# Decode attention and MLP on one core: K1 and V1 are requested in two halves, V1's first half after half of V0

## The chip, the core and the metric

The kernel runs on one core of a Trainium2 chip. The core has a matrix engine (TensorE, PE in the profile, with its weight loads as PEld), a vector engine (VectorE, DVE), a scalar engine (ScalarE, ACT), GpSimd (POOL) and SyncE (SP), which here does nothing but request transfers. Each engine runs its own list of instructions and waits on semaphores. Transfers between the chip's memory and the core's on-chip memory (128 partitions) are done by 16 DMA engines.

The metric is the time of one execution on the device in microseconds (us), the median of several runs.

## The reference

One token is decoded: a layer norm, attention with 32 heads over a cache of 32768 keys and values of 128 numbers each, and a small MLP, each with a residual. Everything is bf16.

```python
def _A_ref(x, k_cache, v_cache, wq, wo):
    B, Sq, D = x.shape            # 1, 1, 512
    H, Dh = 32, 128
    q = (x @ wq).reshape(B, Sq, H, Dh) transposed to (0, 2, 1, 3)
    scores = jnp.einsum("bhqd,bhkd->bhqk", q, k_cache) * (Dh ** -0.5)
    p = _softmax(scores, axis=-1)
    o = jnp.einsum("bhqk,bhkd->bhqd", p, v_cache)
    return o transposed back, reshape(B, Sq, H * Dh) @ wo

def _B_ref(x, w1, b1, w2):        # 512 -> 1376 -> 512
    h = jnp.einsum("bsd,df->bsf", x, w1) + b1
    sp = jnp.log1p(jnp.exp(-jnp.abs(h))) + jnp.where(h > 0, h, jnp.zeros_like(h))
    return jnp.einsum("bsf,fd->bsd", h * jnp.tanh(sp), w2)

h = x + _A_ref(_layernorm(x), k_cache, v_cache, wq, wo)
h2 = h + _B_ref(_layernorm(h), w1, b1, w2)
```

Keys and values of one head are 32768 x 128 x 2 bytes = 8.39 MB each, so the 32 heads read 537 MB.

## The kernel before

**Where data lives.** `ring` holds six slots of 32 KB a partition. Slots 0 and 1 are the home of the keys of even heads, 2 and 3 of odd heads, 4 and 5 of the values of every head. Partition p holds 256 consecutive keys (or values) of a head, "rows" 0 to 255 below, which lie in one run of 64 KB in the chip's memory. The query weights WQ (4.2 MB) lie in slot 4 at the start, so V0 can be requested only when the queries are computed; the output weights WO take the place of the keys of head 30 at the end.

**Requests.** SP goes through a list written out at L446 to L449: WQ, K0, K1, V0, K2, V1, K3, V2, and so on to WO, V31 and the MLP's weights. For each entry it waits until the place is free (L540: for K(h), until TensorE has used K(h-2); for V0, until it has used WQ) and, for V(h) with h > 0, until V(h-1) has been used (L565). `done_with` (L503) names the event waited for: for values it is `pv{h}_64` or `pv{h}_128` if the piece ends at row 64 or 128, and otherwise `pv{h}`, the end of the product with the values. Everything is requested on SP, in this order, and goes into one queue.

**Pieces.** `pieces` (L427) says into which pieces an entry is cut. Before, K0 is cut at row 128 (two pieces with 32 KB a partition), V31 into six pieces, and every other K and V is one transfer with 64 KB a partition. The first piece adds 16 to the semaphore `ready` of the home when it has landed, each later one adds 16 to a semaphore of its own cut, in `cut_sems`. For heads without that cut, SP adds the missing counts itself (L568, L569; `uncut`, L435, says for which heads and how many), so that TensorE, whose code is a loop over heads, can wait for the same count in every round.

**TensorE's rounds.** For each head `head` (L735) runs 32 groups of eight rows: eight transposes of 128 x 128 (L666), a copy by VectorE out of the accumulation memory (L672), and, three groups later, eight products with the query (L642). Then VectorE takes the maximum (L706). `rest` (L746) for head t, after the keys of head t+1, runs C (the sum, L727), the product with the values in four stretches `pv` of rows 0 to 63, 64 to 127 and 128 to 255 (L693; below "pv(t)"), with the next head's small steps A (L712) and B (L717) between them, and `oev`. For head 0 there is a block of its own, `turn` (L741): A0, B0 and the exponential of head 0 stand right after the keys of head 0. So the order on TensorE is keys(0), turn, keys(1), pv(0), keys(2), pv(1), keys(3), and so on. All heads but the first pass run the same instructions again: the loop's blocks are `head` and `rest`.

**What the change touches.** `pieces` (L427 to L430), the semaphores beside L452, the loop on SP that requests keys and values (L561 to L569), and the waits of B in `soft_b` (L716 to L718). A wait named `keys_in` (L76 to L80) makes TensorE wait at the first row of a head's keys until `ready` of that home has its count, 16 per head.

Of the kernel before, what the change touches and what calls it, by code (L numbers as in the profile page):

```python
# [291 lines left out]
def bass_sequential_preLN__mha_block_cached__dense_activation_mish__decode_kernel(  # L292
    nc: bass.Bass,
    A_x: bass.AP,
    A_k_cache: bass.AP,
    A_v_cache: bass.AP,
    A_wq: bass.AP,
    A_wo: bass.AP,
    B_x: bass.AP,
    B_w1: bass.AP,  # L300
    B_b1: bass.AP,
    B_w2: bass.AP,
    out: bass.AP,
):
    build_kernel(nc, A_x, A_k_cache, A_v_cache, A_wq, A_wo, B_w1, B_b1, B_w2, out)


def build_kernel(nc, A_x, A_k_cache, A_v_cache, A_wq, A_wo, B_w1, B_b1, B_w2, out):
# [3 lines left out]
    H = HD // Dh  # L312
# [9 lines left out]
    TPS = 128  # L322
# [19 lines left out]
    def sb(shape, dt, name):  # L342
        cm = nc.sbuf_tensor(name, shape, dt)
        t = cm.__enter__()
        allocs.append(cm)
        return t.ap()
# [21 lines left out]
    gmax = sb([1, 1], F32, "gmax")  # L368
# [39 lines left out]
    sem = nc.alloc_semaphore  # L408
# [3 lines left out]
    ready = [sem(f"ready{i}") for i in range(NS)]  # L412
# [12 lines left out]
    CUTS = {"k": [TPS], "v": [TPS // 2, TPS, 192, 224, 240]}  # L425

    def pieces(what):  # L427
        kind, h = what
        at = CUTS[kind] if what in (("k", 0), ("v", H - 1)) else []
        return list(zip([0] + at, at + [SCOLS]))  # L430

    def cut_at(kind, h, r):
        return r in [r0 for r0, _ in pieces((kind, h))]

    def uncut(what):  # L435


        kind, h = what
        for r in CUTS[kind]:
            if not cut_at(kind, h, r) and (h == 0 or cut_at(kind, h - 1, r)):  # L440
                n = 1
                while h + n < H and not cut_at(kind, h + n, r):
                    n += 1
                yield r, n
# [5 lines left out]
    cut_sems = {k: {r: sem(f"cut_{k}_{r}") for r in CUTS[k]} for k in CUTS}  # L450

    s_wl = sem("wl")  # L452
    w1_sems = [sem(f"w1_{n}") for n in range(len(W1P))]
    w2_sems = [sem(f"w2_{n}") for n in range(len(W2P))]

# [5 lines left out]
    def slot_of(what):  # L461
        if what in HOMES:
            return HOMES[what]
        if what[0] in ("w1", "w2"):
            return HOMES[WL]
        return V_HOME if what[0] == "v" else what[1] % 2 * HALVES
# [6 lines left out]
    def ready_wait(what):  # L473
        if what == WL:
            return (s_wl, 16)
        return (ready[slot_of(what)], 16 * fills[what])

    def free_name(what):
        return "free" + "_".join(map(str, what))

    def freed_by(what):
        if what == WO:
            return done_with("k", H - 2, 0, SCOLS)
        if what[0] == "k" and what[1] > 1:
            return done_with("k", what[1] - 2, 0, SCOLS)
        if what == ("v", 0):
            return [free_name(WQ)]
        return []

    def tiles_of(what):  # L490
        return ring[:, slot_of(what):slot_of(what) + HALVES, :].rearrange("p s (r d) -> p (s r) d", d=Dh)

    def keys_of(cache, h):
        return cache[0, h, :, :].rearrange("(p r) d -> p r d", r=SCOLS)
# [8 lines left out]
    def done_with(kind, h, r0, r1):  # L503
        if kind == "v":
            return [f"pv{h}_{r1}" if r1 in V_EVENTS else f"pv{h}"]
        return [free_name(("k", h, half)) for half in range(HALVES) if r0 < (half + 1) * TPS and r1 > half * TPS]
# [15 lines left out]
    def program(S):  # L522
# [3 lines left out]
        v = nc.vector  # L526
# [4 lines left out]
        def start(dst, src, s):  # L531
            S.dma(SP, lambda: sp.dma_start(dst, src).then_inc(s, 16))  # L532
# [3 lines left out]
        for what in order:  # L536
            slot = slot_of(what)
            if what == ("k", 1):
                S.stay(SP)
            S.wait(SP, freed_by(what))  # L540
            flat = ring[:, slot, :]
            if what[0] == "wq":
                S.wait(SP, ["b1z"])
                start(b1r[0:FJ, :], B_b1[0:FJ * 128].rearrange("(j p) -> j p", j=FJ), s_b1)
                start(b1r[FJ:FJ + 1, 0:FLAST], B_b1[FJ * 128:F].rearrange("(o p) -> o p", o=1), s_b1)
            elif what[0] == "wo":
                start(flat, A_wo.rearrange("(p j) n -> p (j n)", j=32), ready[slot])
            elif what == WL:
                start(wol_v, A_wo[(H - 1) * Dh:H * Dh, :], s_wl)
            elif what[0] == "w1":  # L550
                k = what[1]
                start(w1_v[:, k, :], B_w1[k * 128:(k + 1) * 128, :], w1_sems[k])
            elif what[0] == "w2":
                n = what[1]
                if n + 1 < len(W2_J):
                    j0, j1 = W2_J[n], W2_J[n + 1]
                    start(w2_v[:, j0:j1, :], B_w2[j0 * 128:j1 * 128, :].rearrange("(j p) n -> p j n", p=128), w2_sems[n])
                else:
                    start(w2_v[0:FLAST, FJ, :], B_w2[FJ * 128:F, :], w2_sems[n])
            else:  # L560
                kind, h = what  # L561
                rows = keys_of(A_k_cache if kind == "k" else A_v_cache, h)
                for r0, r1 in pieces(what):
                    if kind == "v" and h:
                        S.wait(SP, done_with(kind, h - 1, r0, r1))  # L565
                    start(tiles_of(what)[:, r0:r1, :], rows[:, r0:r1, :], cut_sems[kind][r0] if r0 else ready[slot])

                for r, n in uncut(what) if kind == "v" else [(r, H - 1) for r in CUTS["k"] if h == 2]:  # L568
                    S.dma(SP, lambda r=r, n=n: sp.sem_inc(cut_sems[kind][r], 16 * n))  # L569
        S.dma(SP, lambda: sp.dma_start(out[0, 0, :].rearrange("(c m) -> c m", c=KC), outr[0:128:32, :]).then_inc(s_out, 16),  # L570
              waits=["fin"])
# [20 lines left out]
        for c in range(2 * KC):  # L592
            cols = xr[0:1, c:D:KC] if c < KC else xr[0:1, (c - KC) * 128:(c - KC + 1) * 128]
            S.step(PE, lambda c=c, cols=cols: t_.matmul(X_REG[:, c:c + 1], cols, identb[0:1, 0:1], start=True, stop=True),
                   name=("xT" if c == 2 * KC - 1 else None), waits=(["identb", (s_x, 16)] if c == 0 else ()))
# [22 lines left out]
        for h in range(H):  # L618
            for kc in range(KC):
# [3 lines left out]
                       name=(["q", free_name(("wq",))] if last else None),  # L623
                       waits=(["xn0", ready_wait(("wq",))] if h == 0 and kc == 0 else ()))
# [90 lines left out]

        def soft_b(h):  # L716
            S.step(PE, lambda: t_.matmul(B_REG, onesm[0:1, :], gmax[:, :], start=True, stop=True),  # L717
                   name=f"B{h}", waits=[f"gmax{h}", "consts0"], kind="B")  # L718
            S.step(DVE, lambda: v.tensor_scalar_mul(nb[:, :], B_REG, -SC), name=f"nb{h}", waits=[f"B{h}"], kind="nb")  # L719

        def soft_exp(h):
# [19 lines left out]
        def turn():  # L741
            soft_a(0)
            soft_b(0)
            soft_exp(0)

        def rest(i):  # L746
            t = i - 1
            soft_c(t)
            pv(t, 0, TPS // 2)
            S.unless_final(PE, "soft_a", lambda: soft_a(i))  # L750
            pv(t, TPS // 2, TPS)
            S.unless_final(PE, "soft_b", lambda: soft_b(i))
            pv(t, TPS, SCOLS)
            oev(t)
            if t < H - 1:
                soft_exp(i)
# [84 lines left out]
    log = {}  # L841
    counted = _Sched(nc, False, events, sems, log)
    program(counted)
    nc.sync.dma_start(ring[:, slot_of(WQ), :], A_wq.rearrange("(p k) n -> p (k n)", k=KC)).then_inc(ready[slot_of(WQ)], 16)
    with nc.Block() as block:
        for eng_name, attr in ((POOL, "gpsimd"), (SP, "sync"), (DVE, "vector"), (ACT, "scalar"), (PE, "tensor")):
            emitter = _Sched(nc, True, events, sems, log, only=eng_name)

            def _run(eng, emitter=emitter):
                program(emitter)  # L850
            getattr(block, attr)(_run)
            assert emitter.cnt == counted.cnt
# [31 lines left out]
```

## Time and profile before

| what | value |
|---|---|
| time, median of 3 runs | 1281.71 us (1281.58 to 1282.12) |
| the profiled execution | 1281.4 us, span of its instructions 1279.6 us |
| mean granted TensorE clock | 0.769 |
| busy: PE, DVE, ACT | 1019.0 us (80%), 716.1 us (56%), 20.8 us (2%) |
| read from the chip's memory | 548.21 MB, 428 GB/s over the span |
| requests of V0, K2, V1, V2 on SP | 16.59, 56.28, 95.31, 127.90 us |

The page divides the span in 40 slices of 32 us; a digit is the busy share in tenths. In the chain of waits each row is a start, a length and what was done or waited for; "issue" is time in which an engine waited for nothing that the profile shows. A row of the windows gives, for a stretch of time, its length, the busy time of PE, PEld, DVE, ACT and POOL with the number of instructions, the granted clock, the share of the DMA engines and the rate in GB/s. In the DMA view, q1 is the queue of SP's transfers and q8 carries instructions; a row gives packets, MB and the share of the 16 engines' time. In the list of waits the numbers are the total, how often, and the longest.

### The profile page before, as it was taken

The page shows a single profiled execution, that of the slowest core. Times are in us where ns is not written, and L with a number is a line of the kernel's source. Part 1 is how long each engine was busy: PE and PEld are TensorE (multiplying, and loading weights), DVE is VectorE, ACT ScalarE, POOL GpSimd, SP SyncE. Part 2 cuts the span into 40 slices and gives each one's busy share as a digit, 9 for nine tenths or more (in the row PEclk, how much of TensorE's full clock was granted, in tenths as well). Part 3 has the DMA queues.
Part 4 walks back from the last instruction along what each step waited for, and adds up shares of the span by engine and source line. Part 5 has one row for each costly group of instructions (what it writes and reads, how often), then busy time and mean ns, then how long its engine had stood idle before and what let it go on. Part 6 is the DMA issues. An engine that isn't in the chain of part 4 may idle for free.

```text
span 1279.6 us, 54437 instructions
## 1 busy us (share of the span) xinstructions
PE 1019.0 (80%) x25044; PEld 992.2 (78%) x25044; DVE 716.1 (56%) x1252; ACT 20.8 (2%) x71; POOL 0.8 (0%) x8
## 2 busy tenths in 40 slices
PE   3699777788777798777797777897777887777987
PEld 3699777788777798777797777897777887777885
DVE  2566654466654566545566544666445666445661
ACT  0000000000000000000000000000000000000000
POOL 0000000000000000000000000000000000000000
PEclk9888777788777788767788776888677887767885
DMA  9979999999999999999999999999999999999998
GB/s 425 420 339 426 445 440 426 426 426 459 426 426 426 449 436 426 426 426 459 426 426 426 453 432 426 426 434 451 426 426 426 457 428 426 426 436 449 426 426 355
DMA packets 12584, 548.35 MB, mean 429 GB/s; under 512 B 1343, under 2 KB 2848, under 8 KB 3616
## 3 DMA queue, kind: packets, MB, share of 16 engines
q1 hardware_dynamic: 12574, 548.22, 99.3%
q8 instruction: 8, 0.13, 0.0%
q10 hardware_dynamic: 2, 0.00, 0.0%
HBM read 548.21 MB, written 0.00 MB: 428 GB/s over the span
## 4 chain that ended last, share of the span: by engine, by line
DMA 55%; DVE 23%; PE 18%; SPq 2%; issue 2%; POOL 0%; POOLq 0%
DMA ring<-in_A_k_cache_dram 54%; DVE ering L672 23%; PE ops L693 9%; PE tps L666 7%; SPq L532 2%; PE sps L642 1%; PE hlp L717 1%; PE hlp L712 1%; DMA ring<-in_B_w_dram 1%; PE hlp L727 0%; PE tps L829 0%; DVE pmax L706 0%; DVE outr L834 0%; DVE gmax L714 0%; SPq L68 0%
## 5 line engine op out<-in xcount | busy, mean ns | idle before, releaser
L666 PE MATMUL tps<-identb,ring 128*128 128x128 bf16 x8192 | 671.1, 233 | 218.4 <-DMA ring<-in_A_k_cache_dram 214.5
L672 DVE COPY ering<-tps 128x1024 bf16<-128x1024 bf16 x1024 | 669.7, 692 | 274.5 <-PE tps L666 274.1
L666 PEld LDWEIGHTS tps<-identb,ring 128*128 x8192 | 524.3, 104 | 221.1 <-issue 221.1
L642 PE MATMUL sps<-qcur,ering 128*128 128x1 bf16 x8192 | 343.9, 164 | 11.3 <-DVE ering L672 6.6
L642 PEld LDWEIGHTS sps<-qcur,ering 128*128 128x128 bf16 x8192 | 309.9, 97 | 14.2 <-DVE ering L672 9.4
L693 PEld LDWEIGHTS ops<-pbuf,ring 128*128 128x128 bf16 x8192 | 226.4, 103 | 15.7 <-issue 12.4
L693 PE MATMUL ops<-pbuf,ring 128*128 128x1 bf16 x8192 | 231.1, 165 | 3.1 <-DMA ring<-in_A_v_cache_dram 2.5
L701 DVE TENSOR_TENSOR oT<-ops,rtotc 128x1 f32 x31 | 5.0, 161 | 107.8 <-PE ops L693 107.8
L714 DVE TENSOR_REDUCE gmax<-hlp 1x1 f32<-1x128 f32 x32 | 8.9, 278 | 63.4 <-PE hlp L712 63.4
L719 DVE TENSOR_SCALAR nbias<-hlp 128x1 f32<-128x1 f32 x32 | 5.1, 158 | 63.5 <-PE hlp L717 63.5
L722 ACT ACTIVATE pbuf<-sps,nbias 128x256 bf16<-128x256 f32 x32 | 15.2, 475 | 1229.4 <-PE ops L693 1171.7
L706 DVE TENSOR_REDUCE pmax<-sps 128x1 f32<-128x256 f32 x32 | 13.6, 425 | 14.3 <-PE sps L642 14.3
L712 PE MATMUL hlp<-ident,pmax 128*1 128x128 f32 x64 | 17.2, 365 | 3.5 <-issue 3.5
L717 PE MATMUL hlp<-gmax,onesmat 1*128 1x1 f32 x64 | 18.5, 356 | 0.4 <-DVE gmax L714 0.4
L717 PEld LDWEIGHTS hlp<-gmax,onesmat 1*128 1x128 f32 x64 | 15.8, 304 | 1.3 <-DVE gmax L714 0.9
L727 PE MATMUL hlp<-esum,onesmat 128*128 128x1 f32 x64 | 12.3, 261 | 5.3 <-issue 2.8
L727 PEld LDWEIGHTS hlp<-esum,onesmat 128*128 128x128 f32 x64 | 9.8, 192 | 7.9 <-issue 7.9
L621 PE MATMUL hlp<-xnT,ring 128*128 128x1 bf16 x128 | 3.5, 165 | 9.1 <-DMA ring<-in_A_wq_dram 9.1
L621 PEld LDWEIGHTS hlp<-xnT,ring 128*128 128x128 bf16 x128 | 3.5, 104 | 9.2 <-issue 9.2
L729 DVE RECIPROCAL rtotc<-hlp 128x1 f32<-128x1 f32 x32 | 5.4, 168 | 4.2 <-PE hlp L727 2.4
L625 DVE CAST qT<-hlp 128x32 bf16<-128x32 f32 x1 | 0.2, 192 | 11.4 <-PE hlp L621 11.4
L722 ACT ACTIVATION_READ_ACCUMULATOR pbuf<-sps,nbias 128x1 f32 x32 | 6.2, 194 | 0.0
(75 smaller groups left out, 37.9 us busy)
## 6 DMA issues: line engine op xcount, KB each, us to landing
ring<-in_A_k_cache_dram SPq DMA_DIRECT2D x2, 4096.0 KB, 26.6
ring<-in_A_v_cache_dram SPq DMA_DIRECT2D x3, 2048.0 KB, 11.3
ring<-in_A_wq_dram SPq DMA_DIRECT2D x1, 4096.0 KB, 12.1
ring<-in_A_wo_dram SPq DMA_DIRECT2D x1, 4096.0 KB, 35.3
ring<-in_B_w_dram SPq DMA_DIRECT2D x4, 344.0 KB, 16.8
ring<-in_A_v_cache_dram SPq DMA_DIRECT2D x1, 1024.0 KB, 14.3
ring<-in_A_v_cache_dram SPq DMA_DIRECT2D x2, 512.0 KB, 15.5
ring<-in_B_w_dram SPq DMA_DIRECT2D x1, 640.0 KB, 16.9
```

Source lines behind the costliest of these rows:

```text
L532: S.dma(SP, lambda: sp.dma_start(dst, src).then_inc(s, 16))
L621: S.step(PE, lambda h=h, kc=kc: t_.matmul(Q_REG[:, h:h + 1], wq_v[:, kc, h * Dh:(h + 1) * Dh], xnT[:, 0, kc:kc + 1], start=(kc == 0), stop ...
L642: S.step(PE, lambda r=r: t_.matmul(S_ps[:, col0 + r:col0 + r + 1], ering[:, bg % NE, r, :], qcur[:, :], start=True, stop=True), name=(name ...
L666: S.step(PE, lambda r=r, at=at: t_.matmul(tb[:, r * 128:(r + 1) * 128], key_tile(S, at), identb[:, :], is_transpose=True, start=True, stop ...
L672: S.step(DVE, lambda: v.tensor_copy(ering[:, bg % NE, :, :].rearrange("p r d -> p (r d)"), tb[:, :]), name=f"ev{bg}", waits=[f"trb{bg}"], ...
L693: S.step(PE, lambda r=r: t_.matmul(o_ps[:, 0:1], vt[:, r, :], pbuf[:, r:r + 1], start=(r == 0), stop=(r == SCOLS - 1)), name=(names or Non ...
L706: S.step(DVE, lambda: v.tensor_reduce(pmax[:, :], S_ps[:, 0:SCOLS], AXX, ALU.max), name=f"pmax{h}", waits=[f"qkh{h}"], kind="pmax")
L712: S.step(PE, lambda: t_.matmul(A_REG, pmax[:, :], ident[:, :], start=True, stop=True), name=f"A{h}", waits=[f"pmax{h}", "ident", f"rcp{h - ...
L714: S.step(DVE, lambda: v.tensor_reduce(gmax[:, :], A_REG, AXX, ALU.max), name=f"gmax{h}", waits=[f"A{h}"], kind="gmax")
L717: S.step(PE, lambda: t_.matmul(B_REG, onesm[0:1, :], gmax[:, :], start=True, stop=True), name=f"B{h}", waits=[f"gmax{h}", "consts0"], kind ...
L722: S.step(ACT, lambda: a.activation(pbuf[:, :], S_ps[:, 0:SCOLS], ACTF.Exp, bias=nb[:, :], scale=SC, accum_out=esum[:, :]), name=f"exp{h}", ...
L727: S.step(PE, lambda: t_.matmul(C_REG, onesm[:, :], esum[:, :], start=True, stop=True), name=f"C{h}", waits=[f"exp{h}"], kind="C")
```

## The change

K1 and V1, one transfer each before, become two with 32 KB a partition. For K1 the first half (rows 0 to 127) adds to a new semaphore `s_k1`, the second to `ready`; TensorE waits for `s_k1` ahead of B0, in the block that runs once. V1's first half waits for `pv0_128`, the product with V0's rows 0 to 127, and adds to `ready`; its second half waits for `pv0`, the end of the product, and adds to the semaphore of the cut at row 128. The counts that SP adds for that cut are then made for head 0 beside V0 and for heads 2 to 30 beside V2, since head 1 has a transfer of its own there.

```diff
     def pieces(what):
         kind, h = what
-        at = CUTS[kind] if what in (("k", 0), ("v", H - 1)) else []
+        at = CUTS[kind] if what in (("k", 0), ("k", 1), ("v", H - 1)) else [TPS] if what == ("v", 1) else []
         return list(zip([0] + at, at + [SCOLS]))
...
     s_wl = sem("wl")
+    s_k1 = sem("k1")
...
                     if kind == "v" and h:
                         S.wait(SP, done_with(kind, h - 1, r0, r1))
-                    start(tiles_of(what)[:, r0:r1, :], rows[:, r0:r1, :], cut_sems[kind][r0] if r0 else ready[slot])
+                    if what == ("k", 1):
+                        s = ready[slot] if r0 else s_k1
+                    else:
+                        s = cut_sems[kind][r0] if r0 else ready[slot]
+                    start(tiles_of(what)[:, r0:r1, :], rows[:, r0:r1, :], s)
...
         def soft_b(h):
             S.step(PE, lambda: t_.matmul(B_REG, onesm[0:1, :], gmax[:, :], start=True, stop=True),
-                   name=f"B{h}", waits=[f"gmax{h}", "consts0"], kind="B")
+                   name=f"B{h}", waits=[f"gmax{h}", "consts0"] + ([] if h else [(s_k1, 16)]), kind="B")
```

## The prediction

> **What bounds the kernel now.** I read the page's slices first, to see which resource is full and where it is not.
>
> ```profile
> span 1279.6 us, 54437 instructions
> DMA  9979999999999999999999999999999999999998
> GB/s 425 420 339 426 445 440 426 426 426 459 426 426 426 449 436 426 426 426 459 426 426 426 453 432 426 426 434 451 426 426 426 457 428 426 426 436 449 426 426 355
> ```
>
> The 16 DMA engines are full in every slice but the third (64 to 96 us) and the last. So the kernel is a stream of 548 MB, and its time is that stream plus whatever time the engines stand empty. The list of waits agrees: TensorE waits for keys once in nearly every head.
>
> ```profile
> PE tps L666 <- DMA ring<-in_A_k_cache_dram: 214.5, 30, 8.8
> ```
>
> These 30 waits, 7.2 us each on average, are TensorE's spare time per head. Next, the chain of waits in order of time, which gives the landings of keys and the place where the stream is held up.
>
> ```profile
> 1.96 21.93 DMA ring<-in_A_k_cache_dram
> ...
> 34.57 2.25 issue
> ...
> 41.86 4.62 issue
> ...
> 57.80 3.06 issue
> ...
> 61.81 0.58 PE hlp L717 x2
> ...
> 88.74 1.80 PE ops L693 x64
> ...
> 91.51 0.59 issue
> 92.10 3.19 PE ops L693 x114
> 95.31 0.33 SPq L532
> ...
> 95.75 40.67 DMA ring<-in_A_k_cache_dram
> ...
> 1175.44 44.77 DMA ring<-in_A_k_cache_dram
> ```
>
> Start plus length is the landing: K0's first half at 23.89 us, K3 at 136.42, K31 at 1220.21. From K3 to K31 lie 56 transfers of 8.39 MB in 1083.8 us: 19.35 us each, 433 GB/s, with no loss. From K0's first half to K3 lie 5.5 transfers (K0's other half, K1, V0, K2, V1, K3): at 19.35 they take 106.4 us and K3 would land at 130.3. It lands **6.1 us** later. That is all that any better order near the start can win; the rest of the span is the stream itself.
>
> Where the 6.1 us go is seen in half-microsecond windows (last column GB/s, the one before it the DMA share; a packet counts where it begins).
>
> ```profile
> 87.00:87.50 0.50, 0.50 (x25) 0.50 (x22) 0.00 (x0) 0.00 (x0) 0.00 (x0) 0.50 3.03 1311
> 88.50:89.00 0.50, 0.50 (x14) 0.33 (x13) 0.22 (x1) 0.00 (x0) 0.00 (x0) 0.50 1.51 655
> 89.00:89.50 0.50, 0.50 (x25) 0.50 (x23) 0.06 (x1) 0.00 (x0) 0.00 (x0) 0.50 0.30 131
> 90.00:96.00 6.00, 4.69 (x151) 4.51 (x147) 0.32 (x2) 0.57 (x2) 0.00 (x0) 0.50 0.00 0
> 96.00:96.50 0.50, 0.35 (x4) 0.36 (x5) 0.00 (x0) 0.00 (x0) 0.00 (x0) 0.50 3.95 1311
> 96.50:97.00 0.50, 0.50 (x8) 0.50 (x6) 0.00 (x0) 0.00 (x0) 0.00 (x0) 0.50 1.77 655
> 97.00:97.50 0.50, 0.50 (x7) 0.50 (x6) 0.28 (x1) 0.00 (x0) 0.00 (x0) 0.50 0.32 131
> ```
>
> 1311 GB/s in 0.5 us is ten 64 KB packets, 655 five, 131 one: the last packet of each of the 16 engines for K2, and the first of each for V1. At 433 GB/s over 16 engines a 64 KB packet takes 2.42 us, so ten engines run dry near 89.7, five near 91.2, one near 91.7, and they resume at 96.25, 96.75 and 97.25: (10 x 6.6 + 5 x 5.6 + 5.6)/16 = 6.2 us empty on average. Two views give the same loss. V1 comes late because it is asked for at 95.31, when V0's last product has ended at 95.29; its packets begin 0.8 us after.
>
> **The change, part by part.** *V1 in two halves.* The first needs only the products of V0's rows below 128. Those end at 88.74 + 1.80 = 90.54, so SP asks at 90.56 instead of 95.31: **4.75 us** earlier. The second half is asked for at pv(0)'s end, about 95.3, behind 9.7 us of the first half (half of 19.35): no gap. On TensorE the wait of pv(1) at row 128 becomes one on a real transfer: V1 as a whole now lands near 111 us (K2's 91.7 and 19.35). Row 128 of pv(1) is reached 3.6 us ahead of its end (114 of 128 such products took 3.19), and the end is at V2's request, 127.9 (row further down), or up to 3.4 sooner by the next paragraph: 9 us or more cover it.
>
> *K1 in two halves.* Its bytes, place in the queue and landing stay; its packets fall from 64 KB to 32 KB. What this moves is TensorE's waiting for "issue" in its first pass, 2.25 and 4.62 us in K1's transfer (23.89 + 9.7 = 33.6 to 53 us). In the DMA view of the stretch 43 to 44 us stands what ends the second one, a 16 KB block of instructions:
>
> ```profile
> q1 hardware_dynamic: 14, 0.92, 211.7%
> q8 instruction: 1, 0.02, 6.7%
> ```
>
> TensorE is back 3 us after; the block has to pass between data packets. 4.62 us is 1.9 packets of 64 KB; with 32 KB packets the same count is 2.3 us, and the first stall goes from 2.25 to 1.1: 3.4 us in all. Bounds: nothing (if the block waits for something else than size) and 10.1, both stalls gone and the clock's fall with them: in the rows below (granted clock ahead of the DMA share) it is halved from the long stall's end to about 53 us, 6.5 us of work of which at most half, 3.2, is lost by it.
>
> ```profile
> 46.00:48.00 2.00, 1.53 (x24) 1.53 (x25) 0.35 (x1) 0.00 (x0) 0.00 (x0) 0.51 1.06 459
> 52.00:54.00 2.00, 2.00 (x42) 2.00 (x40) 1.63 (x3) 0.00 (x0) 0.00 (x0) 0.78 1.23 524
> ```
>
> I take **3.4**, from packet size. Then everything on TensorE up to pv(0) is 3.4 us earlier, V1's first half is asked for near 87.2, and its packets are in the queue at 88.0, before the first engine runs dry at 89.7. It needs only 1.7 of the 3.4. So the whole 6.1 us goes, not 4.75.
>
> The Trainium skill, Runtime: NRT & Kernel Launch, section Instruction fetch mechanics, says that instructions come in 16 KiB blocks over a queue of the engine's own and that a block's cost is mostly hidden. The block size agrees with the row; "mostly hidden" does not, with 4.62 us in plain sight. By the page the K1 half of the change would be worth nothing and the sum would be 4.75.
>
> *Moved late next.* The stall of 0.59 us at 91.51, inside pv(0)'s second half, is a block that was fetched while the data engines were running empty:
>
> ```profile
> q1 hardware_dynamic: 11, 0.07, 15.7%
> q8 instruction: 1, 0.02, 6.6%
> ```
>
> (89 to 90 us, 0.07 MB of data against 0.43 in a full microsecond.) With a full queue it will cost as the others do, 2.3 to 4.6 us, so +1.7 to +4.0. It comes after the request for V1's first half and delays what follows: keys(2), pv(1), the request for V2.
>
> ```profile
> 127.90 0.33 SPq L532 DMA_DIRECT2D ring<-in_A_v_cache_dram  x1
> ```
>
> V2's request goes to 127.9 - 3.4 + 1.7..4.0 = 126.2..128.5, its packets begin at 127.0..129.3. K3 then lands at 130.3 and its first engines run dry 2.0 us before (as K2's did), at 128.3. Loss: 0 to 1.0 on ten engines, at most 0.6 on average; I take **0.3**. From K3 on TensorE waits for keys and everything moves with the stream.
>
> *The small parts.* Two more requests on SP at 0.33 us (the row above): K1's second stands in the queue 30 us before it moves, V1's behind 9.7 us of V1. One wait for K1's first half ahead of B0 on TensorE, in front of nb0, exp0 and keys(1): that half lands near 43.3 (two half transfers after 23.89), B0 runs at 61.81, so 18 us (15 after the shift) cover it. The counts that SP adds by itself move from once to twice, beside waits of tens of us. Keys(1) waits for K1's last byte as before, at 53 us, and starts behind B0, after 58 even with the shift. All at nothing; uncovered, each request would cost its 0.33.
>
> *32 KB packets as such.* The rate of the stretch in which WQ and K0 move, both in 32 KB runs, against that of 64 KB:
>
> ```profile
> 6.00:30.00 24.00, 9.25 (x207) 9.20 (x208) 4.33 (x9) 0.00 (x0) 0.00 (x0) 1.00 1.01 436
> 140.00:540.00 400.00, 325.35 (x8061) 318.49 (x8059) 234.37 (x401) 5.67 (x20) 0.00 (x0) 0.77 1.01 435
> ```
>
> Same rate, price nothing. The dear bound is in the landings: TensorE's first use of WQ starts at 13.01, K0's first half lands at 23.89, 10.9 us for a half transfer, 1.2 over 9.7.
>
> ```profile
> 13.01 3.55 PE L621 MATMUL hlp<-xnT,ring 128*128 128x1 bf16 x128 [9.14 <-DMA ring<-in_A_wq_dram]
> ```
>
> I go with the rate, since a landing also holds how unevenly the engines end.
>
> **Sum.** 6.1 - 0.3 = 5.8 us. The profiled execution took 1281.4 us, 1.8 over its span, and the median is 1281.7; 1281.7 - 5.8 = **1275.9 us**. If keys move at 436 instead of 433 GB/s in the start, K3's loss is 6.7 and the time 1275.0; with the full 0.6 of V2 it is 1276.2, and with less shift than 1.7 it runs into the first rival.
>
> **Rivals.** *K1's halves don't move TensorE.* For it: "issue" names no cause, and one stall took 2.25 and the other 4.62 beside the same packets. Then the request is at 90.56, packets at 91.4, and 1.3 us of the gap stay (6.1 - 4.75). The dearer block in pv(0) puts V2's packets at 128.7 + 1.7..4.0 = 130.4..132.7 against engines dry from 129.7 to 131.7: 0.6 to 2.4 more. Gain 4.2 to 2.4, time **1277.5 to 1279.3**.
>
> *Every half has a price.* If a half transfer takes 10.9 instead of 9.7 us, four of them cost 4.8, and 1281.7 - 5.8 + 4.8 = **1280.7**. The rate over 24 us speaks against it. The Trainium skill, DMA: Bandwidth & Descriptors, section Anatomy of one DMA, gives a DMA a fixed cost of about 2.0 us beside its bytes, which speaks against cutting; if two more DMAs paid it in the open, the time would be about 1279.9. The steady stretch agrees with its remark that most of it is latency at the end: 56 DMAs there lose nothing.
>
> *The block in pv(0) opens a worse gap* (the slower side). It decides when the block's delay, less TensorE's lead, passes about 6.4 us (V2's packets at 128.7 against engines dry at 129.0 on average, plus the 6.1 won). With no lead and two blocks of 4.62 in a row, V2 begins 9.2 us late, 8.9 are lost and 6.1 won: **1284.5**. Against it: no stall in the trace passes 4.62, and only one block is fetched there.
>
> *The lead is given back at the end* by the last V's pieces: **1281.7**. Against it: K31's landing follows K3's without loss, and K31's successors stand in the same queue.
>
> **How the numbers follow.** Chances: forecast 0.76, first rival 0.12, price of halves 0.05, worse gap 0.04, given back 0.03. The range 1274.6 to 1279.2 holds the forecast (1275.0 less the 0.4 that the runs spread) and nearly all of the first rival. About 0.2%, 2.6 us, can be told from no change: faster means below 1279.1. Faster 0.76 + 0.10 = 0.86; same 0.02 + 0.05 + 0.03 = 0.10; slower 0.04.
>
> **What would show it.** Right: the third slice moves 420 GB/s or more; no window near 90 to 96 us without data; V1's first half asked for near 87 and K3 landing at 130 to 131 us; the stall near 42 us at 2 to 3 us. The stalls unchanged and the request at 90.6 is the first rival. A landing of K1 later than 53.5 us is the price of halves. An idle stretch before V2, near 130 us, is the block in pv(0). Wrong altogether: K3 at 130 us, and the end not 5 to 6 us earlier.

## The result and the profile after

The changed kernel takes **1277.43 us** (median of 7 runs, 1276.38 to 1278.50) against 1281.81 us for the kernel before in its 7 runs (1281.55 to 1283.04): 4.4 us less, ratio 0.9964 with a 95% interval of 0.9954 to 0.9974. The profiled execution took 1277.0 us with a span of 1275.2. The forecast was 1275.9 us, 5.8 less.

The page of the changed kernel, its span and the slices:

```profile
span 1275.2 us, 54441 instructions
DMA  9999999999999999999999999999999999999998
GB/s 404 442 412 438 440 432 428 436 434 434 438 430 428 442 432 434 436 428 434 436 434 438 430 428 438 432 434 438 430 432 438 432 440 430 428 438 432 434 416 350
```

The third slice moves 412 GB/s instead of 339 (420 or more was forecast), and its DMA digit is 9 instead of 7. The chain of waits in order of time (start, length, what):

```profile
35.10 0.44 issue
...
40.58 2.15 issue
...
49.17 0.99 issue
...
54.14 4.35 issue
...
59.45 0.58 PE hlp L723 x2
...
86.41 1.80 PE ops L699 x64
...
89.18 0.87 issue
...
93.27 0.33 SPq L533
...
93.71 38.31 DMA ring<-in_A_k_cache_dram
...
1170.65 45.01 DMA ring<-in_A_k_cache_dram
```

K3 lands at 93.71 + 38.31 = 132.02 us, 4.40 earlier than the 136.42 of before, and K31 at 1215.66, 4.55 earlier: what is won near the start reaches the end. B0 (L723) runs at 59.45 instead of 61.81. The requests on SP:

```profile
88.23 5.37 SPq L533 DMA_DIRECT2D ring<-in_A_v_cache_dram  x2
...
125.75 0.33 SPq L533 DMA_DIRECT2D ring<-in_A_v_cache_dram  x1
```

V1's first half is asked for at 88.23, 7.1 us earlier. Half-microsecond windows around the place where 6 us had been empty (DMA share and GB/s last):

```profile
89.00:89.50 0.50, 0.18 (x7) 0.09 (x4) 0.00 (x0) 0.00 (x0) 0.00 (x0) 0.50 0.91 393
89.50:90.00 0.50, 0.00 (x0) 0.00 (x0) 0.00 (x0) 0.00 (x0) 0.00 (x0) 0.50 0.79 262
90.00:90.50 0.50, 0.46 (x17) 0.46 (x18) 0.00 (x0) 0.00 (x0) 0.00 (x0) 0.50 0.98 262
90.50:91.00 0.50, 0.50 (x25) 0.50 (x23) 0.00 (x0) 0.00 (x0) 0.00 (x0) 0.50 0.00 0
91.00:91.50 0.50, 0.50 (x25) 0.50 (x22) 0.00 (x0) 0.00 (x0) 0.00 (x0) 0.50 1.37 590
```

A packet counts where it begins and takes longer than a window, so the last two rows, 0 and 590 GB/s, belong together. No stretch is empty for all engines any more, and yet 1.7 us of the 6.1 are missing: K3 was forecast for 130.3 and landed at 132.02.

The question is where these 1.7 us are. Each transfer adds 16 to its semaphore, one for each DMA engine, and the trace has the time of each increment. The last of the 16 is the landing; from the first to the last is how far the engines lie apart (both worked out from those times, us):

| transfer | before: landing, apart | after: landing, apart |
|---|---|---|
| K0, first half | 23.89, 1.7 | 24.00, 1.9 |
| K1 | 53.17, 1.9 | 53.30, 2.0 |
| V0 | 72.53, 1.9 | 72.65, 2.0 |
| K2 | 91.87, 1.9 | 92.00, 2.0 |
| V1, first half | | 102.99, 2.5 |
| V1 | 117.08, 0.5 | 112.67, 2.5 |
| K3 | 136.41, 0.5 | 132.02, 2.5 |

Two things stand in it. V1's first half lands 10.99 us after K2, 1.3 more than a half transfer's 9.68; every later transfer up to K3 is on time. (The rest of the 1.7 us lies ahead of it: K0's first half lands 0.1 us later than before, and from there to K1's landing it takes 29.3 us, 0.3 more than 1.5 transfers.) And the empty stretch of before had brought the engines level (from 1.9 to 0.5 us), which no longer happens: averaged over the 16 engines K3 is 5.76 us earlier (136.16 to 130.40), but the landing waits for the last engine and is 4.40 earlier.

### The profile page after: what moved, and what is told of

The parts are those of the page before. It is cut to its first block, busy times and chain, and to the rows that moved or that the text cites. A ratio compares the mean times of both kernels' runs of the same rounds, so it can differ in the third digit from the quotient of the medians.

```text
span 1275.2 us, 54441 instructions
## 1 busy us (share of the span) xinstructions
PE 1017.5 (80%) x25044; PEld 991.0 (78%) x25044; DVE 716.3 (56%) x1252; ACT 20.7 (2%) x71; POOL 0.8 (0%) x8
## 4 chain that ended last, share of the span: by engine, by line
DMA 55%; DVE 23%; PE 19%; SPq 2%; issue 2%; POOL 0%; POOLq 0%
DMA ring<-in_A_k_cache_dram 54%; DVE ering L678 23%; PE ops L699 9%; PE tps L672 7%; SPq L533 2%; PE sps L648 1%; PE hlp L723 1%; PE hlp L718 1%; DMA ring<-in_B_w_dram 1%; PE hlp L733 0%; PE tps L835 0%; DVE pmax L712 0%; DVE outr L840 0%; DVE gmax L720 0%; SPq L68 0%
## 5 line engine op out<-in xcount | busy, mean ns | idle before, releaser
L723 PE MATMUL hlp<-gmax,onesmat 1*128 1x1 f32 x64 | 18.5, 357 | 0.4 <-DVE gmax L720 0.4
L723 PEld LDWEIGHTS hlp<-gmax,onesmat 1*128 1x128 f32 x64 | 15.8, 305 | 1.3 <-DVE gmax L720 0.9
L718 PEld LDWEIGHTS hlp<-ident,pmax 128*1 128x1 f32 x64 | 2.7, 81 | 5.4 <-issue 4.9
```

The costliest lines, as they stand in the source:

```text
L718: S.step(PE, lambda: t_.matmul(A_REG, pmax[:, :], ident[:, :], start=True, stop=True), name=f"A{h}", waits=[f"pmax{h}", "ident", f"rcp{h - ...
```

## The experiments

**Theory.** A request has to be made some 3 us before the first engine runs dry, not 0.8; V1's comes 1.8 before, and its landing loses 1.3. K1's halves matter little. **Rivals.** K1's halves give the lead that closes the gap, as forecast; each piece of a transfer has a price; the spread of the engines alone costs the difference. All times below are compared with runs of the kernel before on the same chip.

**e0, the changed kernel again.**

> The changed kernel once more, as the measure for the others. Both theories: 4.4 us under the kernel before (1277.4 us), V1's first half asked for near 88.2 us, K3 landing near 132.0 with about 2.5 us between the first and the last of the 16 engines, where the kernel before has 0.5.

Measured: 1278.08 against 1282.12 us, ratio 0.9968 (0.9956 to 0.9980). V1 asked for at 88.76, V1's first half 1.22 us late, K3 at 132.05 with 2.7 us between the engines. The time is 4.0 us under the kernel before where 4.4 was expected, the landings are as expected. Here V2, asked for at 127.77, lands 0.57 us late as well.

**e1, V1's part alone** (K1 in one transfer, no `s_k1`).

```diff
-        at = CUTS[kind] if what in (("k", 0), ("k", 1), ("v", H - 1)) else [TPS] if what == ("v", 1) else []
+        at = CUTS[kind] if what in (("k", 0), ("v", H - 1)) else [TPS] if what == ("v", 1) else []
```

> V1 in two halves, K1 in one transfer. Theory of the last engine: what counts is when the last engine is served; the empty stretch before V1 used to bring engines that had fallen behind level with the others, and a request needs 2 to 3 us until all engines deliver, so the 2.3 us by which K1's halves bring the request forward are lost again. Then V1's first half is asked for near 90.6, all engines restart together, K3 lands at 136.4 - 4.75 = 131.7 with a spread of 0.5, and the time is that of the changed kernel or up to 0.4 us better (1277.0 to 1277.5). Rival, as predicted: K1's halves are what closes the rest of the gap, and without them 1.1 to 1.6 us are lost: 1278.5 to 1279.0.

Measured: 1277.91 us, ratio 0.9965 (0.9951 to 0.9979), the same as with K1's halves. But not for the reason given. The request on SP, TensorE's waits with B0, and K3's row in the chain of waits:

```profile
88.14 7.27 SPq L532 DMA_DIRECT2D ring<-in_A_v_cache_dram  x2
```

```profile
34.89 1.81 issue
...
43.06 0.96 issue
...
49.10 1.83 issue
...
54.91 3.58 issue
...
59.44 0.58 PE hlp L719 x2
...
95.53 36.41 DMA ring<-in_A_k_cache_dram
```

With K1 in one transfer B0 runs at 59.44, as with K1's halves, so TensorE has its lead in this execution too. V1 is asked for at 88.14, and K3 lands at 131.94. So K1's halves aren't needed for the lead, and the time of the change is V1's.

**e2, K1's part alone** (V1 in one transfer).

```diff
-        ... else [TPS] if what == ("v", 1) else []
+        ... else []
```

> K1 in two halves, V1 in one transfer asked for at the end of pv(0). Both theories: the request moves from 95.3 to 93.0 with TensorE's lead and the empty stretch shrinks by as much, so K3 lands at 134.1 with a spread of 0.5 us (all engines restart together) and the time is 1279.5. If the halves of K1 cost transfer time of their own (rival: each half has a price), K1 lands later than 53.5 and the time is above 1280.5.

Measured: 1281.79 against 1282.12 us, ratio 0.9994 (0.9985 to 1.0003): no difference that can be told, where 1279.5 was expected. Its profiled execution does show what was expected:

```profile
93.53 40.69 DMA ring<-in_A_k_cache_dram
```

K3 at 134.22, the engines 0.5 us apart after the shorter empty stretch, 1279.69 us. Of its 11 executions three took 1279.5 to 1279.7 us, one 1280.8, and seven 1281.7 to 1282.4, as the kernel before. That fits a lead of some 2.2 us which comes in some executions only; the trace is of one of those, and none was kept of a longer one, so it is not shown. K1's transfer itself has no price: from K0's landing at 33.84 to K1's at 53.25 are 19.41 us, 19.57 before.

**e3, V1's first half cut at row 64 as well**, its first piece asked for 1.8 us of products sooner.

```diff
-        ... else [TPS] if what == ("v", 1) else []
+        ... else [TPS // 2, TPS] if what == ("v", 1) else []
```

> Both parts, and V1's first half cut once more at row 64, its first piece asked for when V0's rows 0 to 63 are used, near 86.0. Theory of the last engine, with a request that needs 2 to 3 us: now every engine has V1 in its queue before it runs dry, the 1.3 us that the last engine lost on V1's first half (10.99 us from K2's landing to its own, against 9.68) are gone, K3 lands at 130.7 and the time is 1276.1. Rival, every piece has a price: one more piece makes it 0.5 to 1.2 us worse, 1278 to 1278.6. Rival, the spread of the engines alone costs the difference to the prediction: no change, 1277.4.

SP's requests of V1 and V2, and the landings of K3 and K5 in the chain:

```profile
86.78 8.86 SPq L533 DMA_DIRECT2D ring<-in_A_v_cache_dram  x3
...
127.87 0.33 SPq L533 DMA_DIRECT2D ring<-in_A_v_cache_dram  x1
```

```profile
95.75 35.16 DMA ring<-in_A_k_cache_dram
...
163.06 47.26 DMA ring<-in_A_k_cache_dram
```

K3 lands at 130.91, 1.1 us sooner, as the theory has it: V1's first piece lands 4.89 us after K2, where a quarter transfer takes 4.84. But the time stays at 1277.82 (ratio 0.9962, 0.9948 to 0.9976), because from K3 to K5 lie 79.4 us instead of four transfers' 77.4. V2, asked for at 127.87, 1.0 us before K3's first engine ended, landed 1.64 us late. The gain was given back at the next request. (Of the 2.0 us, the other 0.4 were lost behind V2; no row here says at what.)

**e4, V2 in two halves as well.**

```diff
-        ... else [TPS // 2, TPS] if what == ("v", 1) else []
+        ... else [TPS // 2, TPS] if what == ("v", 1) else [TPS] if what == ("v", 2) else []
```

> As the kernel with V1 cut at rows 64 and 128, and V2 in two halves as well, its first asked for when V1's rows below 128 are used. Theory of the late request (a request must be made some 3 us before the first engine runs dry): V2 is asked for near 124.3 instead of 127.9, 4.6 us before K3's first engines end; the 1.64 us lost between K3 and V2 are gone, V2 lands at 150.3 instead of 151.9, and the time is 1276.2. Rival, pieces cost: 1277.8 or more.

```profile
86.89 9.02 SPq L533 DMA_DIRECT2D ring<-in_A_v_cache_dram  x3
...
124.02 4.34 SPq L533 DMA_DIRECT2D ring<-in_A_v_cache_dram  x2
```

Measured: 1275.85 us (1275.77 to 1276.52) against 1281.61, ratio 0.9960 (0.9947 to 0.9974). V2 lands at 150.50, on time. As expected; more pieces cost nothing.

**e5, V0 in two halves** (to e3's kernel, V2 whole).

```diff
-        ... if what == ("v", 1) else []
+        ... if what == ("v", 1) else [TPS] if what == ("v", 0) else []
```

> As the kernel with V1 cut at rows 64 and 128, and V0 in two halves with 32 KB a partition. Packet size sets TensorE's wait for instructions (as predicted): the wait of 4.4 us at 54 us, beside V0's 64 KB packets, falls to about 2.2, V1 is asked for near 84.6 and V2 near 125.7, so that V2 loses nothing: 1276.2. Rival, the wait has another cause than packet size: it stays above 4 us, V2 is asked for near 127.9, and the time stays at 1277.8.

TensorE's waits in the chain:

```profile
54.87 2.36 issue
...
88.46 1.43 issue
```

The wait beside V0 is 2.36 us instead of 4.43, V1 is asked for at 85.24 and V2 at 125.74, and neither is late. The profiled execution took 1275.58 us; the median is 1276.94 (1275.58 to 1277.41; ratio 0.9967, 0.9954 to 0.9979), halfway between the two expectations: the profiled execution agrees with packet size, the median does not decide.

**e6, the kernel before, one more look.**

> The kernel before, one more look. Theory, TensorE's waits for instructions vary from execution to execution and K1's halves did not make the lead: the three waits differ from 2.25, 4.62 and 3.06 us by more than 1 us in sum, and V1 is asked for up to 2.5 us earlier than 95.3. As predicted (packet size): the same waits within 0.5 us and V1 at 95.3.

```profile
34.14 2.50 issue
...
42.98 3.34 issue
...
52.76 0.56 issue
...
57.30 3.41 issue
...
61.66 0.58 PE hlp L717 x2
```

Measured: 9.8 us of waits in sum against 9.9, V1 asked for at 95.66, 1281.84 us. The sum is as in the first profile, against the theory; the single waits differ by up to 1.3 us, against the expectation from packet size. The kernel before showed no lead in either of its two traces. But of its ten executions beside e4 to e7 three took 1278.92, 1279.74 and 1280.26 us, as a lead of 1.4 to 2.7 us would give; no trace shows those.

**e7, e4 with K1 in one transfer.**

> K1 in one transfer, V1 cut at rows 64 and 128, V2 at row 128. Theory, K1's halves are worth nothing once the requests come early: as the kernel with K1's halves and V2 cut, 1276.2, with V2 landing at 150.3. Rival, K1's halves give TensorE a lead of 2 us that the requests need: V1 asked for near 88.2, 1.3 us lost on V1, 1277.5.

```profile
85.65 7.44 SPq L532 DMA_DIRECT2D ring<-in_A_v_cache_dram  x3
...
121.28 4.34 SPq L532 DMA_DIRECT2D ring<-in_A_v_cache_dram  x2
...
1240.78 7.87 SPq L532 DMA_DIRECT2D ring<-in_A_v_cache_dram  x6
```

Measured: 1275.77 us, ratio 0.9961 (0.9948 to 0.9975), e4's time without K1's halves; V2 at 150.30. Two of its five executions took 1277.35 and 1277.73, and the latter is the profiled one. In it V1 and V2 are on time, and V31's first piece, asked for at 1240.78 with WO's first engine ending at 1241.58, lands 1.77 us late: a third late request.

**e8 and e9, V31's first piece cut at row 32; and with V0 in halves.** K1 stays whole.

```diff
-    CUTS = {"k": [TPS], "v": [TPS // 2, TPS, 192, 224, 240]}
+    CUTS = {"k": [TPS], "v": [TPS // 4, TPS // 2, TPS, 192, 224, 240]}
...
-    V_EVENTS = (TPS // 2, TPS)
+    V_EVENTS = (TPS // 4, TPS // 2, TPS)
...
-        ... else [TPS] if what == ("v", 2) else []
+        ... else [TPS] if what in (("v", 0), ("v", 2)) else []
```

(The last pair is e9's alone.)

> As the kernel with K1 whole, V1 cut at 64 and 128 and V2 at 128, and V31's first piece cut once more at row 32, asked for when V30's rows 0 to 31 are used. Theory of the late request, third place: with V31 asked for only 0.8 us before WO's first engines ended, one profiled execution lost 1.77 us there and ended at 1277.73, while others of that kernel took 1275.6 to 1275.8. Asked for 0.9 us earlier, most of that goes: all executions within 1275.4 to 1276.6, median 1275.7. Rival, the spread of executions has its cause elsewhere (TensorE's waits at the start): executions at 1277.3 and above remain, as 2 of 5 before.

> As the last, and V0 in two halves. TensorE's wait behind the first head's keys, beside V0's packets, falls from 3.5 to about 2.2 us with packets of 32 KB and V1 is asked for near 84 us. Theory: the requests already come early enough, so nothing is left to win near the start: V2 lands at 150.3 and the time is that of the last kernel within 0.4 us, 1275.7. Rival, an earlier TensorE is worth as much again: 1274.5 or less.

e8: 1276.40 us (1275.63 to 1278.11; ratio 0.9961, 0.9947 to 0.9975), with executions of 1277.41 and 1278.11 as the rival had it; V31's late request does not explain all of the longer ones. e9: **1275.78 us** against 1281.85, ratio 0.9952 (0.9938 to 0.9965), all five executions within 1275.69 and 1275.88: 6.07 us less than before. By the intervals it can't be told from e4 and e7 (1275.85 and 1275.77 us), though none of its executions was a longer one. Its wait beside V0 was 3.25 us, not 2.2, and V1 was asked for at 86.77, so in this profile V0's halves moved nothing: e8 without them had 3.00 us and asked at 86.75.

**e10 and e11, e8's kernel twice more**, for a profile of a longer execution.

> The kernel with V31 cut at row 32 once more, for one profile, since some of its executions took 1277.4 to 1278.1 us and others 1275.6 to 1275.8. If this execution is one of the longer ones: with the loss near the start, V1 or V2 lands 1 us or more after K2 or K3 and its transfer time (V1 later than 111.6, V2 later than 150.5); with the loss at the end, V2 lands at 150.3 and V31's first piece more than 2.5 us after WO. If it is a short one, both show nothing.

> The same kernel, a second look, read in the same way: loss near the start shows as V1 later than 111.6 or V2 later than 150.5, loss at the end as V31's first piece more than 2.5 us after WO.

Both were short ones, 1275.72 and 1275.98 us, with nothing late. Where e8's longer executions lose their time stays open.

**What the requests show together.** Lead is from the request to the first engine's end with the transfer ahead; the loss is what the next landing is late by, both from the trace's increments, in us. (An increment comes some 0.5 us after the engine's last data packet: for K2's first engine 90.00 and 89.52, so an engine stands empty that much sooner.)

| request | lead | loss | | request | lead | loss |
|---|---|---|---|---|---|---|
| V1, e0 | 1.2 | 1.2 | | V2, e3 | 1.0 | 1.6 |
| V1, e1 | 1.7 | 1.3 | | V2, e0 | 1.6 | 0.6 |
| V1, after | 1.8 | 1.3 | | V2, e1 | 1.6 | 1.2 |
| V1, e3 and e4 | 3.2 | 0.1 | | V2, e5 | 3.3 | 0 |
| V1, e5 | 5.0 | 0.1 | | V2, after | 3.8 | 0 |

Of these, every request with less than 2 us of lead lost between 0.6 and 1.6 us; from 3.2 on none lost more than 0.1. In the five rows of V2 it is one and the same transfer, in one piece, so its size isn't the reason; and where V1 (e3) and V2 (e4) were cut so as to be asked for sooner, the losses went.

A short lead is a risk, though, and not a fixed price, as V31's first piece behind WO shows. In the changed kernel it was asked for 0.7 us before WO's first engine ended:

```profile
1241.66 7.88 SPq L533 DMA_DIRECT2D ring<-in_A_v_cache_dram  x6
```

It landed on time, as it did in e4, e1 and e3 with leads of 0.9, 1.0 and 1.2 us. The mean of the 16 engines lost 0.4 to 0.6 us there, but those that had run dry did not fall behind the last one: the engines were 2.4 or 2.5 us apart at WO and 1.2 to 1.8 behind it. In e7, with 0.8 us, the landing was 1.77 us late, and in e2, with 2.6, it was 0.3.

## Why the prediction was right, point by point

Of the forecast 5.8 us, 4.4 came. K3 is 1.7 us later than forecast, 1.3 of it at V1's first half, and the 0.3 taken for V2 did not come in the profiled execution: 5.8 - 1.7 + 0.3. The direction and the main cause were right; of the two steps that were to close the rest of the gap, one failed in its mechanism and one in its size. Of the signs that were named for being right, the stall near 42 us came (2.15 us) and the empty stretch went, but the third slice moves 412 GB/s and not 420, and K3 lands at 132.0 and not by 131.

**The 6.1 us at the start were there, nearly all.** With the requests early enough e9 is 6.07 us faster than the kernel before in the medians; in its profile K3 lands at 130.97 us, 5.45 earlier than before and 0.7 behind the 130.3 that was worked out. Of that 0.7, 0.3 is in K1's transfer (19.63 us; it took 19.57 in the kernel before, against 19.35 for a transfer).

**V1's earlier request, 4.75 us: right in kind, and it is the change.** e1 has it alone and gains 4.2 us. The 4.75 by itself was not measured: in e1's profile TensorE's lead is there too, and the request comes 7.2 us earlier (88.14 against 95.31).

**K1's halves, 3.4 us of lead: wrong.** The step took the wait for a block of instructions as a count of packets, 1.9 of them, and from packets half as large a lead that closes the rest of the gap. The waits beside K1 did fall in the profile, from 6.9 to 3.6 us (0.44 + 2.15 + 0.99), but to 5.5 in e0 and, with K1 whole, to 4.6 in e1. And what is saved there is not what B0 gains, because the wait behind keys(0) took part of it back: it was 3.06 us before and 4.35 after (54.14 in the chain), a term that the prediction left as it was. TensorE comes to this wait at 54.0 to 54.9 us with K1's halves and at 54.9 to 55.4 in the changed kernels without them, and leaves it at 58.4 to 58.9 in all of them but e5 (57.2). So B0 runs at 58.2 to 59.8 us in all twelve traces of changed kernels, six of them with K1 whole, and at 61.8 and 61.7 in the two of the kernel before. The lead is 2.3 us, with or without the halves, and by its times e2 mostly lacks it with them. In both traces of the kernel before the third block of instructions starts 9.6 us after the second, beside K1, and in the twelve others 6.4 to 7.4 us (starts of the trace's packets); why stays open. One execution of each kernel could not show that such waits vary. That the request came near the 87.2 us forecast was luck as far as this step goes. The sum 6.1 - 0.3 stood on this lead.

**"Its packets are in the queue before the first engine runs dry": wrong size.** The term was 0.8 us from request to packets, read off engines that stood idle (there the trace has 0.97 for the first and 1.86 for the last). By the prediction's count the lead of 2.3 us was enough, since 1.7 was needed: the request at 88.23 came 1.8 us before the first engine's end at 90.0. Yet 1.3 us were lost. For V1 the need lies between 1.8 and 3.2 us. With the lead of 3.4 that was taken the request would have stood at 87.2, 2.8 us ahead; whether that is enough, no run shows.

**The late block in pv(0), and V2: right in kind, too small.** The wait there rose from 0.59 us to between 2.3 and 2.8 in e0, e1, e3 and e4 (forecast 2.3 to 4.6), and V2 lost up to 1.64 us where 0.6 was the bound, again with its request only 1.0 to 1.6 us ahead of K3's first engine. In the changed kernel's own profile the wait was 0.87 and V2 lost nothing.

**32 KB packets cost nothing: right.** V1's second half took 9.68 us, e2's K1 19.41, and e4's five pieces are free. The price of halves showed nowhere in a full queue. The Trainium skill (DMA: Bandwidth & Descriptors, section Anatomy of one DMA — SWDGE (gpsimd) path) gives a DMA on GpSimd's path a fixed cost of about 2.0 us; for these, requested from SP into a full queue, none showed.

**The slower side** did not occur: no wait of TensorE in the first pass was longer than the 4.62 us of before. The first rival, that K1's halves do not move TensorE, gave 1277.5 to 1279.3. It names the part that failed, and the measured 1277.43 lies at the edge of its span, but by another sum: a lead that comes without the halves, and a request that needs longer.

## What to carry to other kernels

In a kernel that streams like this one, a request was early when it was made some 3 us before the first engine ended (3.2 us and more lost nothing here), and not when it beat the last byte; where the place becomes free in parts, ask for the parts, since pieces of 16 to 32 KB a partition were free here. When one empty stretch is closed, look at the next request in the same queue: here V2's took back what V1's gave, until it was moved as well. Before a wait is explained by its size, look at a second execution of the same kernel.

## What was not expected of the hardware

**A block of instructions puts one DMA engine behind for good.** Each of the seven 16 KB blocks of a first pass took 0.88 to 1.08 us on one engine, and the data packet behind it 0.5 us more than its fellows (1.7 instead of 1.21 us for 32 KB, 2.9 instead of 2.42 for 64 KB): 1.5 us, on another engine nearly every time, for in the changed kernel one engine is late at K0's first half, four at K1, six at V0 and seven at K2. Each transfer is dealt evenly to the 16 engines, so an engine that is behind stays behind: the engines are 2.5 us apart at K3 after the change, still 2.5 at K5. In the kernel before the empty stretch levelled them, from 1.9 to 0.5 us.

**A request into busy engines starts unevenly.** With all engines empty V1's 16 first packets began 0.97 to 1.86 us after the request; asked for at 88.23, while K2 was ending, the first packets of the nine engines that had run dry began 1.5 to 3.3 us after it and took 1.4 to 2.9 us instead of 1.21. The Trainium skill (DMA: Bandwidth & Descriptors, section Latency and other measured facts) gives some 600 ns to the first byte for a request from SP. Counted from the end of the request, which takes 0.33 us, the first of the 16 packets agrees with it on empty engines (0.64 us); the last of them, and all in the second case, are above it.
